# A decode kernel bound by its cache loads: value loads issued from ScalarE's queue, and the result turned by one TensorE transpose

## The chip, the cores and the metric

The kernel runs on one core of one Trainium2 chip. The metric is the device time of one execution in microseconds (us), taken several times. Executions of the kernel before agree within 0.2%.

Words used below. PE is TensorE, PEld its weight load, DVE VectorE, ACT ScalarE, POOL GpSimd and SP SyncE. ACTq and SPq are the queues that these engines issue DMAs from. "k10" is the first of the four key loads of head group 1, "v03" the last value load of head group 0, and so on. The builder is the software that turns the kernel's source into one instruction list for each engine. It may order a list otherwise than the source does, and it decides which of the shared buffers a load gets.

## The reference, cut to what matters

```python
def _A_ref(x, k_cache, v_cache, wq, wo):      # one query position, 32 query heads, 4 cache heads
    q = ...                                    # (x @ wq), 32 heads of 128
    k = jnp.repeat(k_cache, rep, axis=1)       # k_cache, v_cache: 1 x 4 x 65536 x 128, bfloat16
    v = jnp.repeat(v_cache, rep, axis=1)
    scores = jnp.einsum("bhqd,bhkd->bhqk", q, k) * (Dh ** -0.5)
    p = _softmax(scores, axis=-1)
    o = jnp.einsum("bhqk,bhkd->bhqd", p, v)
    return ... @ wo
def _B_ref(x, w_gate, w_up, w_down):           # D = 1024, F = 3584
    return (_gelu(x @ w_gate) * (x @ w_up)) @ w_down
h = x + _A_ref(_layernorm(x), ...)
h2 = h + _B_ref(_layernorm(h), ...)            # returned: 1 x 1 x 1024
```

The caches are 134 MB (2 x 4 x 65536 x 128 x 2 bytes), the weights 39 MB. Each byte is read once.

## The kernel before

All large loads go through `load`. There are five buffers of 4 MB in the pool `chpool`, shared by keys, values and weights. All of these loads are issued from SyncE.

```python
    NBUF = 5
    chpool = ctx.enter_context(tc.tile_pool(name="chpool", bufs=NBUF))
    def load(src, name):
        t = chpool.tile([P, CW], BF16, name=name, tag="ch")
        n, w = src.shape[1], src.shape[2]
        tv = t[:, 0:n * w].rearrange("p (n w) -> p n w", w=w)
        nc.sync.dma_start(out=tv, in_=src)
        return tv
    # ... (cut)
    def kv_dma(src_v, ci, name):               # a load of 4096 KB for every DCH = 4 chunks
        bi, si = divmod(ci, DCH)
        key = (name, id(src_v), bi)
        if si == 0:
            kv_big[key] = load(src_v[:, bi * DCH * CH:(bi + 1) * DCH * CH, :], name)
        tv = kv_big[key] if si < DCH - 1 else kv_big.pop(key)
        return tv[:, si * CH:(si + 1) * CH, :]
```

A key chunk is turned by TensorE (16 transposes a chunk, 64 a load), copied out of PSUM by VectorE (140 of the 256 copies) and ScalarE (116), and multiplied with the queries. A value chunk is 8 products (32 a load). ScalarE also does the exponentials of the softmax.

```python
    def k_chunk_T(g, ci):
        # ... (cut: takes the chunk from kv_dma)
        for c in range(NBK):
            kt_ps = ps_kt.tile([P, NB2, P], F32, name="kt_ps", tag="ktps")
            for b in range(NB2):
                m0 = (c * NB2 + b) * 2 + hf
                nc.tensor.transpose(out=kt_ps[:, b, :], in_=k32s[m0 // 16][:, m0 % 16, :], identity=ident_f[:])
            # ... (cut)
            if act_for(g, ci, c):
                nc.scalar.copy(out=dst_bf, in_=src_bf)
            else:
                nc.vector.tensor_copy(out=dst_bf, in_=src_bf)
    # ... (cut: k_chunk_QK, softmax_head)
    def v_chunk(g, ci):
        st = state[("v", g)]
        v_sb = kv_dma(v_v[g], ci, "v_sb")
        # ... (cut)
        for i in range(GPC):
            a = ci * GPC + i
            c = a % 4
            nc.tensor.matmul(acc[32 * c:32 * c + rep * TG, :], ...,
                             rhs=v_sb[:, i * TG:(i + 1) * TG, :].rearrange("p t d -> p (t d)"), ...)
    # ... (cut)
    for g in range(Hkv):
        for ci in range(NCH + 1):
            if ci < NCH:
                k_chunk_T(g, ci)
            if ci >= 1:
                k_chunk_QK(g, ci - 1)
            if g >= 1 and ci < NCH:
                v_chunk(g - 1, ci)
    for ci in range(NCH):
        v_chunk(Hkv - 1, ci)
```

The values of head group g-1 are worked off beside the keys of group g, since they need the softmax of g-1. At the end the result, 128 x 8, is turned by four 32 x 32 VectorE transposes:

```python
    nc.vector.tensor_tensor(out=o_blk[:, 0:DC], in0=dl_ps[:], in1=hd_cp[:], op=ALU.add)
    for i in range(4):
        nc.vector.transpose(out=o_tr[:, 32 * i:32 * i + 32], in_=o_blk[32 * i:32 * i + 32, :])
    nc.sync.dma_start(out=out[0, 0].rearrange("(c p) -> c p", p=P), in_=o_tr[0:DC, :])
```

## Time and profile before

| what | before | where read |
|---|---|---|
| time, median of 3 | 412.35 us (412.31 to 412.57) | runs |
| span of the profiled run | 410.6 us | page |
| DMA, share of the 16 engines' span | 98.0% in one queue, q1 | page, queues |
| PE / DVE / ACT busy | 66% / 41% / 40% | page, busy time |
| key load, issue to landing | 40.0 us, several deep | page, DMA issues |

These are lines of the page of the kernel before. The DMA line gives the busy tenths of the DMA engines in 40 slices of the span, and below it stands what they moved. A queue's line gives packets, MB and the time that its packets took as a share of 16 engines' span. A group's line ends with its busy time, the mean ns of one instruction, and the idle time of its engine just before them with what ended most of it. A DMA issue's line ends with the median us from issue to landing.

```profile
PE 272.3 (66%) x2576; PEld 193.8 (47%) x2576; DVE 169.5 (41%) x296; ACT 163.0 (40%) x249; POOL 5.1 (1%) x16
...
DMA  8999999999999999999999999999999999999993
GB/s 358 409 456 410 450 414 442 425 436 429 434 433 434 433 429 437 421 444 426 437 427 433 431 431 436 429 425 439 428 437 428 441 426 434 428 433 439 421 422 149
...
q1 hardware_dynamic: 6496, 173.02, 98.0%
...
L289 PE MATMUL acc_ps<-v_sb,pT 128*32 128x512 bf16 x512 | 37.4, 441 | 12.1 <-DMA v_sb<-in_A_v_cache_dram 12.1
...
k_sb<-in_A_k_cache_dram SPq DMA_DIRECT2D x16, 4096.0 KB, 40.0
v_sb<-in_A_v_cache_dram SPq DMA_DIRECT2D x16, 4096.0 KB, 37.6
```

The DMA engines are the limit: 9 in every slice between the first and the last. The time in which the DMA engines moved nothing can be worked out from the page: the queues' shares (98.0% and 0.3%) leave 1.7% of 410.6 us, 7.0 us. That sum is used for all runs below and called the idle DMA time.

### The profile page before, as it was taken

Reading aid. Unit: us, or ns where it says so; the run is one execution under the profiler, and the core shown is the slowest. Engines: PE = TensorE matmul, PEld = TensorE weight load, DVE = VectorE, ACT = ScalarE, POOL = GpSimd, SP = SyncE. Lnnn points to the kernel's source line nnn. Section 1 sums busy time; section 2 is a strip of 40 time slices with the busy share of each in tenths; the row PEclk is TensorE's granted clock in tenths of the full one; section 3 lists DMA queues with packets and bytes.
Section 4 is the critical chain, followed back from the end, with each engine's and each line's share of the span. In section 5 each row is a group of like instructions: output and inputs, shape, how many; then the busy total and the mean of one; then the engine's idle time right before and its main releaser. Section 6 shows DMA issues by size and latency. Waiting matters only on the chain.

```text
span 410.6 us, 6002 instructions
## 1 busy us (share of the span) xinstructions
PE 272.3 (66%) x2576; PEld 193.8 (47%) x2576; DVE 169.5 (41%) x296; ACT 163.0 (40%) x249; POOL 5.1 (1%) x16
## 2 busy tenths in 40 slices
PE   0448888797993938965868399394945536467365
PEld 0227666484673727645565277182822113163134
DVE  0213787766772636751627187344630001021011
ACT  0014676597570748642524775152738000000000
POOL 1000000000000000000000000000020000000000
PEclk9986999969998887996969689979875655556665
DMA  8999999999999999999999999999999999999993
GB/s 358 409 456 410 450 414 442 425 436 429 434 433 434 433 429 437 421 444 426 437 427 433 431 431 436 429 425 439 428 437 428 441 426 434 428 433 439 421 422 149
DMA packets 6682, 173.40 MB, mean 422 GB/s; under 512 B 896, under 2 KB 896, under 8 KB 1152
## 3 DMA queue, kind: packets, MB, share of 16 engines
q1 hardware_dynamic: 6496, 173.02, 98.0%
q8 instruction: 20, 0.33, 0.3%
q14 instruction: 6, 0.05, 0.0%
q10 hardware_dynamic: 160, 0.00, 0.0%
HBM read 173.02 MB, written 0.00 MB: 421 GB/s over the span
## 4 chain that ended last, share of the span: by engine, by line
DMA 51%; PE 21%; ACT 5%; DVE 4%; issue 1%; DVEq 0%
DMA k_sb<-in_A_k_cache_dram 27%; PE kt_ps L216 13%; DMA wu_sb<-in_B_w_up_dram 10%; DMA v_sb<-in_A_v_cache_dram 10%; DMA wd_sb<-in_B_w_down_dram 5%; ACT pT L272 4%; PE qk_ps L239 3%; PE acc_ps L289 2%; ACT kt_sb L220 2%; DVE mx L246 1%; PE wu_ps L158 1%; DVE kt_sb L222 1%; DVE sc_sb L245 1%; PE o_ps L305 1%; PE bc_ps L262 0%
## 5 line engine op out<-in xcount | busy, mean ns | idle before, releaser
L216 PE MATMUL kt_ps<-ident_f,k_sb 128*128 128x128 f32 x1024 | 144.7, 304 | 37.2 <-DMA k_sb<-in_A_k_cache_dram 34.2
L216 PEld LDWEIGHTS kt_ps<-ident_f,k_sb 128*128 128x128 f32 x1024 | 131.7, 159 | 57.8 <-issue 36.5
L220 ACT COPY kt_sb<-kt_ps 128x1024 bf16<-128x1024 bf16 x116 | 111.9, 1015 | 105.4 <-issue 74.7
L222 DVE COPY kt_sb<-kt_ps 128x1024 bf16<-128x1024 bf16 x140 | 95.3, 688 | 92.8 <-PE kt_ps L216 89.8
L272 ACT ACTIVATE pT<-sc_sb,nbias 128x256 bf16<-128x256 f32 x64 | 47.6, 745 | 23.7 <-DVE nbias L264 23.7
L239 PE MATMUL qk_ps<-kt_sb,qsel 128*32 128x512 bf16 x512 | 39.7, 384 | 9.9 <-ACT kt_sb L220 9.2
L289 PE MATMUL acc_ps<-v_sb,pT 128*32 128x512 bf16 x512 | 37.4, 441 | 12.1 <-DMA v_sb<-in_A_v_cache_dram 12.1
L246 DVE TENSOR_REDUCE mx<-sc_sb 128x8 f32<-128x512 f32 x32 | 35.2, 1099 | 0.5
L245 DVE STREAM_TRANSPOSE sc_sb<-qk_ps 128x512 f32<-128x512 f32 x32 | 23.0, 717 | 19.1 <-PE qk_ps L239 18.8
L289 PEld LDWEIGHTS <-pT 128*32 128x32 bf16 x512 | 17.2, 107 | 28.4 <-issue 19.7
L165 ACT COPY wg_ev<-wg_ps 96x512 f32<-96x512 f32 x1 | 0.6, 582 | 59.3 <-PE wg_ps L158 59.3
L239 PEld LDWEIGHTS <-qsel 128*32 128x32 bf16 x512 | 8.4, 94 | 24.4 <-DVE kt_sb L222 15.2
L298 PE MATMUL l_ps<-lpart,ones_f 128*128 128x8 f32 x16 | 3.8, 312 | 21.7 <-ACT pT L272 21.7
L298 PEld LDWEIGHTS l_ps<-lpart,ones_f 128*128 128x128 f32 x16 | 3.2, 250 | 24.0 <-ACT pT L272 23.1
L158 PEld LDWEIGHTS <-hnz 128*32 128x32 bf16 x112 | 5.2, 131 | 17.6 <-issue 16.0
L158 PE MATMUL wu_ps<-wu_sb,hnz 128*32 128x512 bf16 x56 | 7.2, 625 | 8.8 <-DMA wu_sb<-in_B_w_up_dram 8.8
L353 PE MATMUL at_ps<-wo_sb,o2z 128*32 128x512 bf16 x64 | 7.2, 629 | 8.3 <-DMA wo_sb<-in_A_wo_dram 8.3
L302 DVE COPY acc_sb<-acc_ps 128x512 f32<-128x512 f32 x4 | 2.7, 684 | 22.6 <-PE acc_ps L289 22.6
L272 ACT ACTIVATION_READ_ACCUMULATOR pT<-sc_sb,nbias 128x1 f32 x64 | 12.0, 187 | 0.0
L165 ACT ACT_TABLE_LOAD x1 | 1.3, 1283 | 25.9 <-DVE q_ev L163 25.9
L125 PE MATMUL ln_tot<-ln_s,ones_f 128*128 128x1 f32 x4 | 1.2, 362 | 13.8 <-DVE ln_s L123 13.8
L353 PEld LDWEIGHTS <-o2z 128*32 128x32 bf16 x64 | 2.7, 139 | 12.0 <-issue 11.5
(107 smaller groups left out, 93.5 us busy)
## 6 DMA issues: line engine op xcount, KB each, us to landing
k_sb<-in_A_k_cache_dram SPq DMA_DIRECT2D x16, 4096.0 KB, 40.0
v_sb<-in_A_v_cache_dram SPq DMA_DIRECT2D x16, 4096.0 KB, 37.6
wq_sb<-in_A_wq_dram SPq DMA_DIRECT2D x2, 4096.0 KB, 16.8
wo_sb<-in_A_wo_dram SPq DMA_DIRECT2D x2, 4096.0 KB, 43.1
wg_sb<-in_B_w_gate_dram SPq DMA_DIRECT2D x2, 3584.0 KB, 43.5
wu_sb<-in_B_w_up_dram SPq DMA_DIRECT2D x2, 3584.0 KB, 40.6
wd_sb<-in_B_w_down_dram SPq DMA_DIRECT2D x1, 3584.0 KB
wd_sb<-in_B_w_down_dram SPq DMA_DIRECT2D x1, 1792.0 KB, 29.7
```

What stands on the lines that cost most here:

```text
L158: nc.tensor.matmul(banks[s // 4][32 * g:32 * g + 32, :], lhsT=stat, rhs=mov(s), start=first, stop=last, tile_position=(0, 32 * g))
L216: nc.tensor.transpose(out=kt_ps[:, b, :], in_=k32s[m0 // 16][:, m0 % 16, :], identity=ident_f[:])
L220: nc.scalar.copy(out=dst_bf, in_=src_bf)
L222: nc.vector.tensor_copy(out=dst_bf, in_=src_bf)
L239: nc.tensor.matmul(qk_ps[32 * c:32 * c + 32, :], lhsT=qsel[:, g, par, hf, :], rhs=mv[:, :, 32 * c:32 * c + 32, par], start=(hf == 0 and pa ...
L245: nc.vector.transpose(out=sl.rearrange("p n h -> p (n h)"), in_=qk_ps[:])
L246: nc.vector.tensor_reduce(out=st["mx"][:, :, pi], in_=sl.rearrange("p n h -> p h n"), axis=AX.X, op=ALU.max)
L272: nc.scalar.activation(out=pT[:, :, r, :], in_=sc_sb[:, hf * HG * TG:(hf + 1) * HG * TG, r].rearrange("p (a t) -> p a t", t=TG), func=ACT. ...
L289: nc.tensor.matmul(acc[32 * c:32 * c + rep * TG, :], lhsT=pTs[a // HG][:, a % HG, :, :].rearrange("p r t -> p (r t)"), rhs=v_sb[:, i * TG: ...
L298: nc.tensor.matmul(l_ps[:], lhsT=ones_f[:], rhs=lpart[:, hf, :], start=(hf == 0), stop=(hf == NH - 1))
L305: nc.tensor.matmul(o_ps[:], lhsT=acc_sb[:, t * Dh:(t + 1) * Dh], rhs=sel[:, t:rep * TG:TG], start=(t == 0), stop=(t == TG - 1))
L353: nc.tensor.matmul(bank[32 * g:32 * g + 32, :], lhsT=stat, rhs=w2[:, s * 512:(s + 1) * 512], start=first, stop=last, tile_position=(0, 32 ...
```

## The change

The intent: key and value loads issued from two queues, so that neither stands behind the other in one list, and a shorter end.

```diff
-    def load(src, name):
+    def load(src, name, queue=None):
         ...
-        nc.sync.dma_start(out=tv, in_=src)
+        (queue or nc.sync).dma_start(out=tv, in_=src)
         ...
         if si == 0:
-            kv_big[key] = load(src_v[:, bi * DCH * CH:(bi + 1) * DCH * CH, :], name)
+            kv_big[key] = load(src_v[:, bi * DCH * CH:(bi + 1) * DCH * CH, :], name,
+                               nc.scalar if name == "v_sb" else nc.sync)
         ...
-    nc.vector.tensor_tensor(out=o_blk[:, 0:DC], in0=dl_ps[:], in1=hd_cp[:], op=ALU.add)
-    for i in range(4):
-        nc.vector.transpose(out=o_tr[:, 32 * i:32 * i + 32], in_=o_blk[32 * i:32 * i + 32, :])
-    nc.sync.dma_start(out=out[0, 0].rearrange("(c p) -> c p", p=P), in_=o_tr[0:DC, :])
+    nc.vector.tensor_tensor(out=o_col[:], in0=dl_ps[:], in1=hd_cp[:], op=ALU.add)
+    oT_ps = ps_t.tile([DC, P], BF16, name="oT_ps", tag="T")
+    nc.tensor.transpose(out=oT_ps[:], in_=o_col[:], identity=ident_bf[:])
+    o_row = rows.tile([DC, P], BF16, name="o_row")
+    nc.vector.tensor_copy(out=o_row[:], in_=oT_ps[:])
+    nc.sync.dma_start(out=out[0, 0].rearrange("(c p) -> c p", p=P), in_=o_row[:])
```

More of the change, by code (lines that the diff above doesn't have):

```diff
@@ L445 @@
     nc.vector.memset(dl_ps[:], 0.0)
-    o_blk = rows.tile([P, 32], BF16, name="o_blk")
-    nc.vector.memset(o_blk[:], 0.0)
-    o_tr = rows.tile([32, P], BF16, name="o_tr")
+    o_col = rows.tile([P, DC], BF16, name="o_col")
     c0 = 0
```

## The prediction

> **What bounds it.** The DMA engines. The page's slices show them 90% or more busy from slice 2 to 39; the queue part gives one queue, q1, 98.0% of the engines' span for 173.02 MB. At the steady rate of the slices (about 432 GB/s) a 4096 KB load takes 9.7 us and all bytes 400 us of the 410.6 us span: no reordering can win more than about 2%. PE is 66%, ACT 40%, DVE 41% busy. A key load is worked off in about 11 us, a value load in 2, a softmax head in about 10 (PE timeline): some 70 us per head group against 78 us of its DMA. Compute has modest slack.
>
> **What the change moves.** The 16 value loads leave SyncE's in-order list for ScalarE's. Bytes, buffers (5) and copies stay.
> 1. Issue cost: 0.33 us each on SyncE. On ScalarE 16 x 0.33 = 5 us against 163 us of work, spread out; PE's waits for DMA (37 us before the transposes) absorb it. 0 to 1 us.
> 2. ScalarE could block on a buffer's release. Value issues follow the last transposes of an older key load (SyncE's waits name kt_ps), and ScalarE's next copies come from later transposes of the same PE list, so I expect waits of 1 us or less. The builder visibly rearranged the order (l_ps products long before the last value products), so I expect value issues near those moments, not behind the softmax as in the source.
> 3. Order of landing. Before: first in, first out, issue to landing about 40 us, four loads deep. The Trainium skill ("DMA: Bandwidth & Descriptors", Queues, rings and completion order) says SyncE and ScalarE each have one ring on the same 16 engines, and an engine alternates between rings by packet; no run here shows it yet. Rows of both kinds are 32 KB, so I assume halves. No bandwidth is added; the first value load (issued at 43 us) overtakes and delays keys by some 6 to 15 us in head group 0, which the slack regains.
> 4. The tail. At 300.6 us 3.5 value loads are outstanding when wo is issued. In one queue values land first (the last at 336.4). With halves, wo and wg overtake: I work out the last value landing about 20 us later, near 358, when wo and wg have mostly landed. What follows is a serial chain (acc, o, wo, norm, gate, up, down), 58 us in the PE timeline once its DMA waits are removed. It then ends last instead of the DMA: span 358 + 58 = 416, about 6 us longer.
> 5. Output: four 0.20 us DVE transposes become a PE transpose (0.3, as mxT) and a DVE copy (0.2): saves 0.2 to 0.3 us, all on the path.
>
> **Predicted time:** 417 us, 8 in 10 between 411.5 and 430. Faster by over 2%: 0.01; within 2%: 0.67; slower by over 2%: 0.32.
>
> **What would show it.** Queue q10 carrying 67 MB, same total bytes, mean near 417 GB/s; in group 0 key loads take longer from issue to landing than values; last value landing after 350 us; PE's waits for wo, wu and wd gone from the chain of waits, which becomes PE, DVE and ACT after the last value product; the last DMA slices emptier; ACT busy time unchanged.
>
> **What would make it wrong.** The engines may serve one ring more than the other: with 40% for values I work out 15 us more, with 60% nothing. The builder may order buffers differently, letting keys or weights take them first, or put value issues where ScalarE stalls behind them: tens of us.

## More of the kernel before

The order on TensorE, from its timeline (start, duration, line, operation, count; in brackets the idle time before it and what ended it):

```profile
97.05 1.91 PE L289 MATMUL acc_ps<-v_sb,pT 128*32 128x512 bf16 x32
...
99.33 1.97 PE L216 MATMUL kt_ps<-ident_f,k_sb 128*128 128x128 f32 x16
...
110.42 1.93 PE L289 MATMUL acc_ps<-v_sb,pT 128*32 128x512 bf16 x32
```

Here the builder has grouped the work: all 32 products of v00 in one piece (97.05), then the transposes of k11, 16 at a time, then all 32 products of v01 (110.42). SyncE's timeline of the same time:

```profile
99.01 0.33 SPq L93 DMA_DIRECT2D k_sb<-in_A_k_cache_dram  x1
108.83 0.33 SPq L93 DMA_DIRECT2D v_sb<-in_A_v_cache_dram  x1
```

The last product of v00 ends at 98.96 (97.05 + 1.91), and less than 0.1 us later the load k13, which takes its buffer, is issued. Every load of this kernel stands like that. The measure used below is lateness: the start of a load's issue in the trace, less the end of the last TensorE instruction that read the former load of the same buffer (which buffer a load has is read from the built program). In the kernel before it is at most 0.1 us for each of the 16 value loads.

## The result, and the profile after

The changed kernel took 424.35 us (median of 4, 423.16 to 424.62) against 412.42 us of the kernel before (median of 4): slower, by 11.9 us. The ratio is 1.0284, with a 95% interval of 1.0268 to 1.03. A ratio is the mean time of one kernel's fast runs over that of the other's of the same rounds, so it is not quite the ratio of the medians that are quoted.

The same lines of the page after:

```profile
PE 285.2 (68%) x2577; PEld 172.5 (41%) x2577; DVE 163.6 (39%) x292; ACT 164.1 (39%) x249; POOL 5.1 (1%) x16
...
DMA  8999999999799999996999999879999999999995
GB/s 348 444 410 436 445 432 414 442 436 419 300 447 445 419 425 436 436 416 259 412 435 441 432 418 439 365 323 421 447 393 432 434 426 436 431 431 435 431 422 215
...
q1 hardware_dynamic: 4192, 105.91, 58.9%
q10 hardware_dynamic: 2464, 67.11, 37.0%
...
L290 PE MATMUL acc_ps<-v_sb,pT 128*32 128x512 bf16 x512 | 55.0, 526 | 67.0 <-DMA v_sb<-in_A_v_cache_dram 55.5
...
k_sb<-in_A_k_cache_dram SPq DMA_DIRECT2D x16, 4096.0 KB, 24.1
v_sb<-in_A_v_cache_dram ACTq DMA_DIRECT2D x16, 4096.0 KB, 20.8
```

Four things are to be seen. First, the bytes are the same (105.91 + 67.11 = 173.02 MB), and the span has 11.6 us more (422.2). The shares of the queues leave 3.8% of the span idle, 16.0 us instead of 7.0, so 9.0 us of the 11.6 are DMA engines with nothing to do; the packets themselves took 2.6 us more (the shares are rounded, so each of these is good to about half a microsecond). Second, the idle time is not at the end: it lies in slices 11, 19 and 26 to 27 (300, 259, 365 and 323 GB/s), where one head group passes to the next. Third, issue to landing is nearly halved, 24.1 and 20.8 us instead of 40.0 and 37.6. That looks like an improvement, but it only says that fewer loads stand in line: two kernels below that use the same two queues and lose nothing have 40.7 and 37.5 us (f2) and 30.9 and 26.3 us (f5). Fourth, TensorE waits 55.5 us for value loads instead of 12.1. That number is the most tempting one of the page, and the experiments show that it is not what the change cost.

Look at the first hole. This is the windows view from 108 to 112 us (length; busy time of PE, PEld, DVE, ACT and POOL; granted clock; DMA share; GB/s), of the kernel before and then of the kernel after:

```profile
108.00:112.00 4.00, 3.36 (x56) 1.90 (x54) 3.19 (x5) 1.93 (x2) 0.00 (x0) 1.00 1.04 451
```

```profile
108.00:112.00 4.00, 3.11 (x21) 1.28 (x24) 0.00 (x0) 1.01 (x1) 0.00 (x0) 0.50 0.53 193
```

Half of the DMA engines' time is empty. One of the five buffers lay free and unfilled at that moment, and another was held for the sake of four transposes, as the timelines show. TensorE of the kernel after:

```profile
93.26 2.43 PE L290 MATMUL acc_ps<-v_sb,pT 128*32 128x512 bf16 x24 [1.73 <-ACT pT L273]
...
96.02 1.04 PE L290 MATMUL acc_ps<-v_sb,pT 128*32 128x512 bf16 x8
108.89 1.01 PE L290 MATMUL acc_ps<-v_sb,pT 128*32 128x512 bf16 x5 [11.83 <-DMA v_sb<-in_A_v_cache_dram]
109.83 1.12 PE L217 MATMUL kt_ps<-ident_f,k_sb 128*128 128x128 f32 x4
```

The list is not grouped any more. The last four transposes of k10 (109.83) stand behind products of v01 (108.89), and v01 had not landed: TensorE stood still for 11.83 us, with k10 landed since 76.0 and all but worked off. SyncE shows what hung on those four transposes: the load k13, which takes the buffer of k10.

```profile
110.98 0.33 SPq L93 DMA_DIRECT2D k_sb<-in_A_k_cache_dram  x1
```

ScalarE of the kernel after, around 65 us and around 117 us, has the other half:

```profile
61.79 1.93 ACT L221 COPY kt_sb<-kt_ps 128x1024 bf16<-128x1024 bf16 x2 [0.52 <-ACT kt_sb L221]
...
65.12 0.36 ACTq L93 DMA_DIRECT2D v_sb<-in_A_v_cache_dram  x1
...
110.99 1.01 ACT L221 COPY kt_sb<-kt_ps 128x1024 bf16<-128x1024 bf16 x1 [9.12 <-PE kt_ps L217]
116.75 1.93 ACT L221 COPY kt_sb<-kt_ps 128x1024 bf16<-128x1024 bf16 x2 [4.76 <-PE kt_ps L217]
117.71 0.34 ACTq L93 DMA_DIRECT2D v_sb<-in_A_v_cache_dram  x1
```

The issue at 65.12 is v00. It takes the buffer of k00, whose last transpose ended at 42.6, so it is 22.5 us late, and not for want of ScalarE's time: ScalarE idles between the copies ahead of it. It is late because it stands behind copies of later keys in the list. The issue at 117.71 is v02. Its buffer, that of v00, was free at 97.1; but the copies ahead of it (110.99, 116.75) wait for transposes that stand behind the products of v01, which wait for a value load that was itself issued 8.1 us late (73.1). The Trainium skill says that the queues of ScalarE, VectorE and GpSimd "are strict FIFO" ("PSUM — Partial Sum Buffer", Engine vs sequencer instructions); this trace agrees, down to a DMA issue that comes 20.6 us after its buffer is free, behind copies that it does not need, the last two of which themselves waited 9.12 and 4.76 us for TensorE.

Over the 16 value loads the lateness sums to 134 us (before: 0.5): 22.5, 8.1, 20.6, 9.2, 0, 0, 6.9, 9.2, 0, 0.1, 7.0, 9.2, 13.3, 7.5, 8.6 and 11.1.

### The profile page after: what moved, and what is told of

Read it like the earlier page. It is cut to its first block, busy times and chain, and to the rows that moved or that the text cites. A ratio compares the mean times of both kernels' runs of the same rounds, so it can differ in the third digit from the quotient of the medians.

```text
span 422.2 us, 5997 instructions
## 1 busy us (share of the span) xinstructions
PE 285.2 (68%) x2577; PEld 172.5 (41%) x2577; DVE 163.6 (39%) x292; ACT 164.1 (39%) x249; POOL 5.1 (1%) x16
## 3 DMA queue, kind: packets, MB, share of 16 engines
q1 hardware_dynamic: 4192, 105.91, 58.9%
q10 hardware_dynamic: 2464, 67.11, 37.0%
HBM read 173.02 MB, written 0.00 MB: 410 GB/s over the span
## 5 line engine op out<-in xcount | busy, mean ns | idle before, releaser
L221 ACT COPY kt_sb<-kt_ps 128x1024 bf16<-128x1024 bf16 x116 | 113.1, 1013 | 137.0 <-PE kt_ps L217 114.2
L217 PE MATMUL kt_ps<-ident_f,k_sb 128*128 128x128 f32 x1024 | 148.3, 289 | 22.4 <-DVE kt_sb L223 18.3
L217 PEld LDWEIGHTS kt_ps<-ident_f,k_sb 128*128 128x128 f32 x1024 | 114.7, 145 | 74.6 <-DVE kt_sb L223 35.4
L223 DVE COPY kt_sb<-kt_ps 128x1024 bf16<-128x1024 bf16 x140 | 93.6, 681 | 88.9 <-PE kt_ps L217 79.1
L290 PE MATMUL acc_ps<-v_sb,pT 128*32 128x512 bf16 x512 | 55.0, 526 | 67.0 <-DMA v_sb<-in_A_v_cache_dram 55.5
L290 PEld LDWEIGHTS <-pT 128*32 128x32 bf16 x512 | 15.9, 116 | 91.3 <-issue 75.7
L158 PE MATMUL q_ps<-wq_sb,xnz 128*32 128x512 bf16 x64 | 6.8, 599 | 3.1 <-DMA wq_sb<-in_A_wq_dram 2.1
L301 DVE RECIPROCAL rl<-l_ps 128x8 f32<-128x8 f32 x4 | 0.8, 207 | 16.5 <-PE l_ps L299 16.5
L306 PE MATMUL o_ps<-sel,acc_sb 128*128 128x8 f32 x32 | 5.0, 285 | 2.7 <-DVE acc_sb L303 2.4
L125 PEld LDWEIGHTS ln_tot<-ln_s,ones_f 128*128 128x128 f32 x4 | 1.0, 312 | 13.9 <-DVE ln_s L123 13.9
## 6 DMA issues: line engine op xcount, KB each, us to landing
k_sb<-in_A_k_cache_dram SPq DMA_DIRECT2D x16, 4096.0 KB, 24.1
v_sb<-in_A_v_cache_dram ACTq DMA_DIRECT2D x16, 4096.0 KB, 20.8
```

Of the source, the lines that this page charges most:

```text
L158: nc.tensor.matmul(banks[s // 4][32 * g:32 * g + 32, :], lhsT=stat, rhs=mov(s), start=first, stop=last, tile_position=(0, 32 * g))
L290: nc.tensor.matmul(acc[32 * c:32 * c + rep * TG, :], lhsT=pTs[a // HG][:, a % HG, :, :].rearrange("p r t -> p (r t)"), rhs=v_sb[:, i * TG: ...
L306: nc.tensor.matmul(o_ps[:], lhsT=acc_sb[:, t * Dh:(t + 1) * Dh], rhs=sel[:, t:rep * TG:TG], start=(t == 0), stop=(t == TG - 1))
```

## The experiments

Theories. A: the value issues come late in ScalarE's list, and lateness alone costs the time. B: two rings share the engines, so keys or the last values land later, whoever issues (the tail of the prediction). C: the issue itself costs ScalarE time. D: the builder's mixed TensorE list costs the time by itself. And E, which came last: lateness and mixed list together. The expectations, quoted below, use the letters otherwise: at first their theory A is late issues or a mixed list or both, and from f4 on their theory C is what is called E here. Edits are shown against the kernel before if nothing else is said. All thirteen gave correct results.

| run | edit in words | median us | ratio to before | idle DMA us |
|---|---|---|---|---|
| e1_queue_only | value loads on ScalarE's queue | 424.35 | 1.0291 [1.0253, 1.033] | 16.5 |
| e2_output_only | the output alone | 412.07 | 0.9992 [0.9977, 1.0007] | 6.6 |
| e3_gpsimd_queue | value loads on GpSimd's queue | 413.75 | 1.0033 [1.001, 1.0057] | 7.4 |
| e4_act_early | e1, issues moved up in the source | 416.66 | 1.0094 [1.0076, 1.0112] | 10.8 |
| e7_act_pinned | e4, later copies kept behind the issues | 413.98 | 1.0039 [1.0021, 1.0058] | 6.2 |
| f1_fixed_sp | grouped list held, SyncE | 412.48 | 1.0001 [0.9987, 1.0016] | 7.0 |
| f2_fixed_act | grouped list held, ScalarE | 412.29 | 0.9996 [0.9981, 1.0011] | 6.6 |
| f3_late2 | f2, issues two chunks later | 413.74 | 1.0021 [1.0005, 1.0038] | 7.4 |
| f4_mixed_sp | mixed list held, SyncE | 412.41 | 0.9999 [0.9982, 1.0015] | 7.0 |
| f5_mixed_act | mixed list held, ScalarE | 412.59 | 1.0007 [0.9992, 1.0022] | 6.6 |
| f6_mixed_late2 | f5, issues two chunks later | 480.81 | 1.168 [1.1628, 1.1731] | 69.4 |
| f7_after_fixed | f2 with the output half | 411.87 | 0.9986 [0.9971, 1.0001] | 6.6 |
| r1_replay_early | the changed kernel's own lists, issues moved up | 415.55 | 1.0071 [1.0054, 1.0088] | 9.1 |

The median of before was 412.44 in the rounds of e1 to f7 and 412.32 in those of r1.

### The two halves apart: e1_queue_only and e2_output_only

e1 has only the part of the change above that is in `load` and `kv_dma`; e2 has only the part at the end:

```diff
+            kv_big[key] = load(..., name, nc.scalar if name == "v_sb" else nc.sync)     # e1
```

```diff
-        nc.vector.transpose(out=o_tr[:, 32 * i:32 * i + 32], in_=o_blk[32 * i:32 * i + 32, :])
+    nc.tensor.transpose(out=oT_ps[:], in_=o_col[:], identity=ident_bf[:])               # e2
+    nc.vector.tensor_copy(out=o_row[:], in_=oT_ps[:])
```

> Only the queue half of the change. Theory A (orders: value issues stand late in ScalarE's list and TensorE's list mixes value products among key transposes, so buffers lie empty or are held and the DMA engines run dry at head boundaries) and theory B (the sharing of the engines by two rings costs by itself) both expect the whole loss here: 424.5 us, within 0.5 of the full change. If it is under 420, the output half costs something, against both.

> Only the output half. Both theories: 0.2 to 0.3 us under the kernel before, 412.1 to 412.3 us; buffers, lists and DMA as before.

e1 measured 424.35 us: the queue is the whole loss. e2 measured 412.07, 0.37 us under before, a gain that the ratio's interval does not tell from none. The timelines do show it. The end of before, then that of e2:

```profile
407.67 0.84 DVE L467 STREAM_TRANSPOSE o_tr<-o_blk 32x32 bf16<-32x32 bf16 x4
408.58 0.36 SPq L468 DMA_DIRECT2D out_dram<-o_tr  x1
```

```profile
407.65 0.27 PE L465 MATMUL oT_ps<-ident_bf,o_col 128*8 128x128 bf16 x1 [0.26 <-DVE o_col L463]
407.95 0.21 DVE L467 COPY o_row<-oT_ps 8x128 bf16<-8x128 bf16 x1 [0.36 <-PE oT_ps L465]
408.24 0.36 SPq L468 DMA_DIRECT2D out_dram<-o_row  x1
```

The last addition starts at 407.47 before and at 407.43 in e2, so from there to the issue of the result it is 1.11 us before and 0.81 in e2: 0.30 us saved.

### Another queue, not ScalarE's: e3_gpsimd_queue

```diff
+            kv_big[key] = load(..., name, nc.gpsimd if name == "v_sb" else nc.sync)
```

> Value loads on a second queue whose engine (GpSimd) has nothing else in its list. Theory A: value issues within 2 us of their buffer's release, so less idle DMA than after; TensorE's list is still mixed in this build (value products in groups of 8 between key transposes), so 412 to 419 us. Theory B: two rings still share, so 422 us or more.

413.75 us. Here too two queues share the engines, the last value load lands at 360.6 us (361.4 in the changed kernel, 336.4 before), and TensorE waits 70.4 us for value loads, longer than in the changed kernel. But GpSimd has nothing else in its list at that time, every value load is issued 0.3 us after its buffer is free, and nearly all of the loss is gone. So sharing the engines (B) is not the cause, nor is TensorE's wait for values as such.

### Issues moved up in the source: e4_act_early, and with the copies kept behind them: e7_act_pinned

```diff
+    plan = [...]                    # the load order of the kernel before
+    def next_load():                # issues the next load of the plan, values on nc.scalar
+        ...
     def k_chunk_T(g, ci):
         ...
+        if ci % DCH == DCH - 1:     # the last chunk of a key load: its buffer comes free
+            next_load()
     def v_chunk(g, ci):
         ...
+        if ci % DCH == DCH - 1:
+            next_load()
```

e7 adds, against e4:

```diff
-                nc.scalar.copy(out=dst_bf, in_=src_bf)
+                with tc.issue_after(pinned[-1]) if pinned else ExitStack():   # the last value issue
+                    nc.scalar.copy(out=dst_bf, in_=src_bf)
```

> Value loads on ScalarE's queue, but written in the source at the place where their buffer is released, so that they should stand earlier in ScalarE's list. The TensorE list is still mixed as in the full change. Theory A: value issues mostly within 2 us of release (after: 0 to 22 us), time between 413 and 421; if lateness falls and the time stays above 421, then the mixed TensorE list is the larger part of A. Theory B: 424 us, whatever the lateness.

> As the run with early written value loads on ScalarE (which measured 416.7 us, its first value issue still 22 us late), with the following ScalarE copies forced behind each value issue; TensorE's list keeps its mixed order and the buffers the order of the full change. Theory A with lateness as the main part: 412 to 415 us. If the time stays at 416 to 417, the rest of the loss belongs to the mixed list or the order of buffers, not to lateness. Theory B: 424 us (already doubtful).

e4 measured 416.66 us and e7 413.98. The builder does not keep the source's order: in e4 the first value load was still 22.5 us late (sum of lateness 90 us), in e7 0.1 us (sum 55). The loss falls with the lateness, 11.9, 4.2 and 1.5 us for 134, 90 and 55, which speaks for A. But the rest of the lists moved too from kernel to kernel, so these two alone don't settle it.

### Lists held by hand, one queue against two: f1_fixed_sp and f2_fixed_act

The builder is kept from ordering TensorE's and ScalarE's lists; the source's order is made the grouped one, a value load's 32 products in one piece after whole key loads. The two kernels differ in the queue of the value loads. Their TensorE lists and their buffers are identical, ScalarE's lists but for the 16 issues; VectorE's list is not held, and a few of its 296 instructions stand elsewhere.

```diff
+    with tc.manual_schedule(engines={mybir.EngineType.PE, mybir.EngineType.Activation}):
         for g in range(Hkv):
             for ci in range(NCH + 1):
                 ...
+                if ci < NCH and ci % DCH == DCH - 1:
+                    next_load()                    # f1: values on nc.sync; f2: on nc.scalar
                 ...
+                if g >= 1 and ...:                 # after each whole key load
+                    for j in range(b * DCH, (b + 1) * DCH):
+                        v_chunk(g - 1, j)
+                    next_load()
```

> Control: all loads on SyncE, TensorE's and ScalarE's lists held to the order written in the source, which has the load order, the buffers and the block order (64 transposes of a key load, then 32 products of a value load) of the kernel before. Both theories: 410 to 414 us, DMA idle time as before (9.5 us of the span, all at its ends).

> The control with the value loads on ScalarE's queue, at their buffer's release in ScalarE's list; TensorE's list and the buffers are instruction for instruction those of the control. What is left is the sharing by two rings and 16 issues on ScalarE. Theory A (late issues and held buffers): within 3 us of the control, value issues at most 2 us late. Theory B (two rings): 422 us or more.

412.48 and 412.29 us: no difference, and none to before. (The 9.5 us of idle DMA time in the first expectation is not the sum used here, which is 7.0 us for before and for f1.) This is the same queue change as e1 at no cost at all. f2 has every effect of the two rings that the prediction feared. Its page, its TensorE timeline, and the share of the queues between 332 and 352 us:

```profile
DMA  8999999999999999999999999999999999999993
...
q1 hardware_dynamic: 4192, 105.91, 60.1%
q10 hardware_dynamic: 2464, 67.11, 38.0%
```

```profile
359.09 3.60 PE L301 MATMUL acc_ps<-v_sb,pT 128*32 128x512 bf16 x32 [16.62 <-DMA v_sb<-in_A_v_cache_dram]
...
398.27 2.49 PE L375 MATMUL d_ps<-wd_sb,actz 128*32 128x512 bf16 x28 [3.51 <-DMA wd_sb<-in_B_w_down_dram]
```

```profile
q1 hardware_dynamic: 153, 4.40, 50.9%
q10 hardware_dynamic: 145, 4.23, 49.1%
```

The two queues take halves. The Trainium skill says that SyncE and ScalarE each own one ring on each of the same 16 engines and that an engine goes round-robin between rings by packet ("DMA: Bandwidth & Descriptors", Queues, rings and completion order); the halves in this trace agree with that. The first value load lands at 67.4, and k10, which in before landed at 72.5, lands at 89.2. The last value load lands at 359.1, where before had 336.4, and TensorE waits 16.62 us for it. And yet the kernel is not slower, because the DMA engines never ran dry and the last weight bytes land when they did: 406.8 us, against 407.0 before. TensorE still has to wait for them (3.51 us at 398.27). B and C fall here. Nor does the second queue make the packets themselves slower: span less idle time is 403.8 us in f2 and 403.6 in before, but 406.2 in the changed kernel. Where those 2.6 us come from stays open.

### Late issues on the grouped list: f3_late2

Against f2, the value issues come two key chunks later in ScalarE's list. TensorE's list is identical to f2's.

```diff
+    LATE = 2
             if name == "v_sb":
-                kv_big[...] = load(..., nc.scalar)
+                held.append([LATE, tv, src])       # the buffer is taken now, the issue comes later
+    def issue_held():                               # after each key chunk's copies
+        ...
+            nc.scalar.dma_start(out=tv, in_=src)
```

> As the run before, but each value load's issue stands two key chunks (some 5 us) later in ScalarE's list; the builder then hands out buffers in the same order as in the full change at the start (the third value load takes the first one's buffer). TensorE's block order is unchanged, its products are not mixed. Theory A: slower than the unlate one by 4 to 12 us, with idle DMA near the head boundaries (around 110, 190 and 270 us). If it stays within 2 us, lateness alone does not make the loss and the mixed TensorE list is needed for it.

413.74 us, 1.3 us over before (the interval lies above 1), and less than the 4 us at least that was expected of theory A. The lateness sums to 165 us, more than the 134 of the changed kernel, at a ninth of its loss. TensorE waited 65.9 us for values. So A, lateness alone, falls: late issues are covered as long as the DMA engines have another load in line, and here they did (idle 7.4 us).

### The mixed list: f4_mixed_sp, f5_mixed_act and f6_mixed_late2

Here 8 value products follow each key chunk, so that value products and key transposes are mixed as in the changed kernel's list, but regularly. The TensorE lists of the three are identical. f4 issues from SyncE and f5 from ScalarE, both on release; f6 is f5 with the same delay by two chunks as f3.

```diff
-                if g >= 1 and ...:                 # f1, f2: after each whole key load
-                    for j in range(b * DCH, (b + 1) * DCH):
-                        v_chunk(g - 1, j)
-                    next_load()
+                if g >= 1 and ci < NCH:            # f4, f5, f6: after each key chunk
+                    v_chunk(g - 1, ci)
+                    if ci % DCH == DCH - 1:
+                        next_load()
```

> All loads on SyncE, as in the control, but TensorE's list holds 8 value products after every 16 key transposes (control: 32 after 64). Revised theory C: the loss needs both a late value load and a TensorE list in which its products stand between the key transposes, so that the key buffer is held while TensorE waits. Here no load is late: 411 to 415 us. Rival D (the mixed list costs by itself): 418 us or more.

> The mixed TensorE list with the value loads on ScalarE's queue at their buffer's release (same TensorE and VectorE lists as in the run on SyncE). C: 411 to 416 us, as the run on GpSimd's queue with its mixed list (413.8). D, or two rings together with a mixed list: 418 us or more.

> The mixed list with each value issue two key chunks late in ScalarE's list; the same lateness with the grouped list cost 1.3 us (413.7). C: both together give the loss of the full change: 419 to 428 us, TensorE waits for value loads of 50 us or more, DMA idle around the head boundaries. If it stays under 416 us, C falls too, and the exact lists of the full change matter in a way that I have not named.

f4 and f5 took 412.41 and 412.59 us: mixing alone costs nothing, so D falls for this regular mix (for the changed kernel's own mix see r1), although TensorE waits 53.3 and 56.0 us for values, just as in the changed kernel (55.5). f6 took 480.81 us. The direction was expected, the size was not, by far. The two factors form a square:

| | issued on release | issued two chunks late |
|---|---|---|
| grouped TensorE list | f2: 412.29 us | f3: 413.74 us |
| mixed TensorE list | f5: 412.59 us | f6: 480.81 us |

Either alone is free or nearly so, both together cost 68 us. Two things limit the square. "Two chunks late" is a place in ScalarE's list and not a time: the lateness sums to 165 us in f3 and to 303 us in f6, where it feeds itself. And in the built programs the late column also hands out the buffers otherwise: there most value loads take the buffer of a value load and keys that of a key load, on the left they take each other's. So the rows differ in the buffers too; in each column both kernels have the same. No run splits this for f6; r1 below, where the buffers of the loads stay put, splits it for the changed kernel. The page of f6, then its TensorE timeline and its ScalarE timeline around one value load:

```profile
DMA  8999999999959779594949788594559999999995
...
q1 hardware_dynamic: 4192, 105.91, 51.5%
q10 hardware_dynamic: 2464, 67.11, 33.8%
```

```profile
204.08 0.62 PE L268 MATMUL qk_ps<-kt_sb,qsel 128*32 128x512 bf16 x8
215.81 1.04 PE L316 MATMUL acc_ps<-v_sb,pT 128*32 128x512 bf16 x8 [11.11 <-DMA v_sb<-in_A_v_cache_dram]
216.78 3.68 PE L245 MATMUL kt_ps<-ident_f,k_sb 128*128 128x128 f32 x16
```

```profile
196.85 0.33 ACTq L225 DMA_DIRECT2D v_sb<-in_A_v_cache_dram  x1
...
218.84 1.01 ACT L249 COPY kt_sb<-kt_ps 128x1024 bf16<-128x1024 bf16 x1 [13.63 <-PE kt_ps L245]
...
224.04 0.33 ACTq L225 DMA_DIRECT2D v_sb<-in_A_v_cache_dram  x1
```

This is a closed loop. v11 is issued at 196.85, 22.6 us after its buffer was free. TensorE waits for it until 215.81. Only behind its products come the next key transposes (216.78), behind those ScalarE's copies (218.84), and behind the copies the issue of v12 at 224.04, now 23.4 us late, because its buffer was free at 200.6. The loop takes 27.2 us (224.04 - 196.85), and in it one key load and one value load are moved, 8.39 MB. At the 432 GB/s of the slices they take 19.4 us, an estimate from these numbers, so the engines stand idle for the rest. In f3 the loop does not close. These are its issue of v12 and its products of v11:

```profile
191.38 0.33 ACTq L225 DMA_DIRECT2D v_sb<-in_A_v_cache_dram  x1
```

```profile
196.07 1.91 PE L316 MATMUL acc_ps<-v_sb,pT 128*32 128x512 bf16 x32 [1.75 <-DMA v_sb<-in_A_v_cache_dram]
```

Here v12 was issued at 191.4, while v11 was still on its way (landed at 196.0), because the transposes and copies ahead of that issue do not stand behind v11's products in TensorE's list. So a second value load was in line. The 16 transposes after the wait also took 3.68 us, and 1.97 where TensorE came from work (99.33 in the kernel before).

### Both halves with the lists held: f7_after_fixed

f2 plus the output half of the change, the diff of e2.

> Both halves of the change with the lists held as in the run that measured 412.3 us. All theories that put the loss into the lists: 411.8 to 412.2 us (412.3 less the 0.3 us of the output half), so about the kernel before less 0.4 us.

411.87 us (411.8 to 412.02), the lowest median of all, at 0.9986 of before with an interval that just holds 1. So the change can be had without loss, and what it gains is the output's 0.3 us or little more (the medians differ by 0.57). The bytes leave no more to win: the DMA engines were idle for 6.6 us of this run's 410.1.

### The changed kernel's own lists, only the issues moved: r1_replay_early

The square above is made of hand-held lists. r1 is the test on the real ones. The lists of TensorE and VectorE are fixed exactly as the builder had made them for the changed kernel, and SyncE's came out the same; ScalarE's list is the same but for the 16 value issues, which are moved up to where their buffers come free. The buffers of the loads are the same; which PSUM buffer a transpose writes is not always. The diff is against the changed kernel:

```diff
+    there = {i.name: i for i in nc.cur_bb.bb.instructions}
+    for text in ('136 146 153 ...', '120 121 124 243 ...', '106 107 233 ...'):   # the lists of PE, DVE, ACT
+        names = ...
+        for a, b in zip(names, names[1:]):
+            tc.add_manual_dep(there[b], a, ...)    # order only: b after a
```

> The full change with TensorE's, VectorE's and SyncE's lists and the buffers held exactly as they are in it; only the 16 value issues are moved up in ScalarE's list, to the first copy whose transposes come after the buffer's release. Theory C (the loss is the loop: a late issue stands behind key copies that stand behind the value products of an earlier load): at most 416 us, value issues within 7 us of release, little idle DMA before the end. If the mixed list alone were the cause it stays at 420 to 425 us.

415.55 us. The lateness falls to 1.0 us in sum, and the loss from 11.9 to 3.2 us. The issue of v00 stands at 42.77 us instead of 65.12, and the busy tenths of the DMA engines lose the holes but for one:

```profile
42.77 0.36 ACTq L93 DMA_DIRECT2D v_sb<-in_A_v_cache_dram  x1
```

```profile
DMA  8999999999899999999999999999999999999994
```

So on the changed kernel's own lists, the place of 16 DMA issues in ScalarE's list is worth 8.8 us (424.35 - 415.55, medians of two groups of runs; 8.7 when each is taken against the kernel before of its own rounds). The rest of 3.2 us belongs to the rest of the changed lists and buffers. In the window from 108 to 112 us r1 moves more than the changed kernel but not what before does:

```profile
108.00:112.00 4.00, 4.00 (x34) 1.34 (x30) 0.69 (x1) 4.00 (x12) 0.00 (x0) 0.61 0.76 254
```

The last column is 254 GB/s, against 193 and 451. I did not split those 3.2 us further by a run; of the 3.8 us that r1's profiled span is longer than that of before (414.4 and 410.6), 2.1 are idle DMA time (9.1 and 7.0). Nor did I test why the builder ordered the lists of the changed kernel so. And r1 tells what moving the issues is worth, not how often the loop of f6 turns in the changed kernel: one turn was followed there, from v01 to v02.

## Why the prediction was right or wrong, point by point

The forecast was 417 us, so 4.65 us more than the 412.35 of the kernel before, and 11.9 came. "Slower by over 2%" was given a chance of 0.32 and is what happened. The measured time lies in the stated range, but the cause that the forecast was built on is not the one that acted.

**What bounds it: right.** f1, f2, f4 and f5 have two TensorE lists, each on one queue and on two, and end within 0.2 us of the 412.44 of before, all with 6.6 to 7.0 us of idle DMA time.

**Step 1, issue cost on ScalarE: right.** f2 issues all 16 from ScalarE and loses nothing.

**Step 2, ScalarE's waits: this is the step that failed.** It said "I expect waits of 1 us or less" and "I expect value issues near those moments, not behind the softmax as in the source". The waits at the issues were small indeed, but the wrong thing to ask for: the issues do not block, they are blocked. They stood up to 22.5 us after the moments named, 134 us in sum, behind key copies in the same list. And the builder mixed value products into the key transposes on TensorE, so that those copies waited for the very values that were late. What this costs was measured on the kernel's own lists: 8.8 of the 11.9 us (r1). The prediction did write "put value issues where ScalarE stalls behind them" down among the risks, with "tens of us", but put no part of it in the sum.

**Step 3, landing order: right in mechanism, and harmless.** Halves were assumed; f2 shows 50.9% and 49.1%. In f2 k10 lands 16.7 us later than before (89.2 - 72.5), a little above "6 to 15 us", and the slack does regain it. In the changed kernel it hardly happened, since v00 was issued too late to overtake k10, which landed at 76.0.

**Step 4, the tail: the landing was right, the cost was not.** "The last value landing about 20 us later, near 358" came true: 359.1 in f2, 361.4 in the changed kernel. But "it then ends last instead of the DMA: ... about 6 us longer" was 0 us. What follows the last value load took 51.3 us in f2 (410.4 - 359.09), not 58, and 3.51 us of that is still a wait for weights: without it the chain is 47.8 us, 10 less than the forecast had. In these three kernels the end follows the last weight bytes: 3.6 us after them before (410.6 - 407.0), 3.6 in f2 (410.4 - 406.8) and 3.3 in the changed kernel (422.2 - 418.9). The forecast's 4.65 us came nearly all from this term, which cost nothing, while what did cost 8.8 us had no term in the sum. That the forecast pointed to a slower kernel at all was luck.

**Step 5, output: right.** "Saves 0.2 to 0.3 us"; 0.30 in the timelines of e2.

**What would show it.** Queue q10 with 67 MB: right (67.11). Keys in group 0 longer on their way than values: right (50.0 us for k10 and 24.4 for v00 in the changed kernel, 46.9 and 38.8 before). Mean near 417 GB/s: 411. "PE's waits for wo, wu and wd gone": wrong, TensorE still waited 7.6 us for wu in the changed kernel and for wd in f2. "The last DMA slices emptier": the last slice is fuller (215 GB/s instead of 149), and the holes are in the middle. ACT busy time unchanged: right (163.0 and 164.1 us).

What was left out of the whole forecast is the loop: a load's issue was treated as an event of the DMA queue, when in the changed kernel it is an instruction in the list of an engine whose other work depends on what that load brings.

## What to carry to other kernels

When a DMA issue moves to a compute engine, ask which instructions stand ahead of it in that engine's list, and what those wait for; if the answer leads back to a load of the same kind, late issues feed themselves. Lateness (issue less release of the buffer) and the idle time of the DMA engines tell this apart from a long but harmless wait of TensorE: 56 us of waiting cost nothing in f5, and 55.5 us went with 12 us of loss in the changed kernel. Loads that must follow a buffer's release belong on an engine with nothing else in its list (e3: 413.75 us), or in a list that is held by hand (f2: 412.29 us).

## What the Trainium skill lacked or had wrong

- "DMA: Bandwidth & Descriptors", Issuing engines are not separate DMA queues, says that issuing from several engines only saves the sequencer's time to initiate a DMA. As to bandwidth the runs agree (f1 412.48, f2 412.29 us). It lacks what the issuing engine's list can cost: 424.35 us in the changed kernel and 480.81 in f6, because the issue stands behind work that waits for the loads. The rules at the page's end call spreading DMAs over engines no help, and have no warning that it can harm.
- The same page, Where 436 GB/s comes from, says that for transfers between HBM and SBUF the HBM side, about 358 GB/s per core, binds. Here one core read HBM into SBUF at 421 GB/s over its whole span and at 430 and more in 21 of the 40 slices. The page's own note under its measured table, that the numbers there (up to 425) are of one core with the pair's other core idle, fits; the sentence on what binds does not.
- "PSUM — Partial Sum Buffer", Engine vs sequencer instructions, has the strict order of ScalarE's list, and the trace agrees. That section doesn't say what the order means for a DMA issue that stands in it: v02's issue came 20.6 us after its buffer was free, behind copies that waited for TensorE.
